# Window attention on one core: patch loads moved from Sync to GpSimd, loads of x moved from GpSimd to Sync

## The chip, the cores and the metric

The kernel runs on one core of a Trainium2 chip. The metric is the device time of one execution in microseconds (us), lower is better. The fast runs of one kernel in one batch agree (the kernel before, seven runs: 5340.21 to 5358.49 us), so times are medians, and two kernels are compared on runs made on the same chip in the same batch. A run counts as fast when it lies within 1.5 per cent of the fastest of its kernel; where a kernel was run only once, its state is unknown, and that is said. PE is the matmul engine, DVE VectorE, ACT ScalarE, POOL GpSimd and SP SyncE. SP only issues transfers here.

## The reference, cut to what matters

```python
# x: [1, 511, 511, 192] bf16, windows of 7x7 (73 x 73 = 5329 of them), 4 heads
pe = 0
for i in range(3):
    for j in range(3):
        pe = pe + xp[:, i:i+H, j:j+W, :] * dw_pe[i, j]   # depthwise 3x3, x padded by 1
x0 = x + pe
h = layernorm(x0)
qkv = windows(h) @ w_qkv                  # per window: 49 tokens x 192
out = softmax(q @ k^T * dh**-0.5) @ v     # per head
return x0 + out @ w_o
```

Of the kernel before, what the change touches and what calls it, by code (L numbers as in the profile page):

```python
# [33 lines left out]
def _window_attn_kernel(ctx: ExitStack, tc: tile.TileContext, x, dw_pe, w_qkv, w_o, out, fast=None, eps=1e-5, logit_lim=40.0):  # L34
    nc = tc.nc
# [55 lines left out]
    def segments(blk):  # L91
        n0 = blk * BLK
        n1 = min(n0 + BLK, NWIN)
        segs = []
        n = n0
        while n < n1:
            a, b0 = divmod(n, NWC)
            b1 = min(NWC, b0 + (n1 - n))
            segs.append((a, b0, b1, n - n0))
            n += b1 - b0  # L100
        return segs

    def load_xc(blk):
        xc = XC[blk % 2]
        for (a, b0, b1, p0) in segments(blk):
            for o in range(0, b1 - b0, 16):
                nb = min(16, b1 - b0 - o)
                nc.gpsimd.dma_start(  # L108
                    out=xc[p0 + o : p0 + o + nb].rearrange("p (r q) c -> p r (q c)", q=WS), in_=xw[a, b0 + o : b0 + o + nb]
                )  # L110

    def load_xp(blk):
        for (a, b0, b1, p0) in segments(blk):
            nb = b1 - b0
            if a == NWR - 1 and blk > 0:
                nc.gpsimd.memset(XP[0:KP, p0 : p0 + nb, :], 0.0)
            else:
                if b0 == 0:
                    nc.gpsimd.memset(XP[0:9, p0 : p0 + 1, :], 0.0)
                if b1 == NWC:  # L120
                    nc.gpsimd.memset(XP[64:KP, p0 + nb - 1 : p0 + nb, :], 0.0)
            pr0 = 1 if a == 0 else 0
            pr1 = 8 if a == NWR - 1 else 9
            h0 = WS * a - 1
            for pc in range(9):
                if pc == 0:
                    q, sh = WS - 1, -1
                elif pc == 8:
                    q, sh = 0, 1
                else:  # L130
                    q, sh = pc - 1, 0
                bb0, bb1 = b0, b1
                if pc == 0 and bb0 == 0:
                    bb0 = 1
                if pc == 8 and bb1 == NWC:
                    bb1 = NWC - 1
                if bb1 <= bb0:
                    continue
                nc.sync.dma_start(
                    out=XP[9 * pc + pr0 : 9 * pc + pr1, p0 + bb0 - b0 : p0 + bb1 - b0, :],  # L140
                    in_=xr[h0 + pr0 : h0 + pr1, bb0 + sh : bb1 + sh, q, :],
                )


    load_xc(0)
    load_xp(0)

    nc.gpsimd.memset(Sel, 1.0)
# [85 lines left out]
    def main(fast):  # L234
      with ExitStack() as mctx:
# [344 lines left out]
        if NBLK > 1:  # L580
            load_xp(1)
# [5 lines left out]
        for g in range(NGL + LE + 1):  # L587
# [9 lines left out]
            if ck == LE and blk >= 1:  # L597
                proj(blk - 1)
                store(blk - 1)
                if blk + 1 < NBLK:  # L600
                    load_xc(blk + 1)
# [3 lines left out]
            if nb < NBLK:  # L605
                if blk == 0 and ck == 0:
                    load_xc(nb)
# [5 lines left out]
                if ck == cend and nb + 1 < NBLK:  # L613
                    load_xp(nb + 1)
# [75 lines left out]
```

## The kernel before: the parts that the change and the argument touch

A block is 128 windows; there are 42. x is loaded twice. Once by token into `XC`, with one window on each partition (this is the x that the convolution is added to). Once as patches into `XP`: the 9x9 patch of a window lies on 81 partitions, so that the depthwise convolution is one small matmul per channel. A patch load fills nine neighbouring partitions (nine rows of the image, one column of the patch) for up to 73 windows, with 384 bytes per window and partition.

```python
def load_xc(blk):                                  # x by token, 9 or 10 loads a block
    xc = XC[blk % 2]
    for (a, b0, b1, p0) in segments(blk):
        for o in range(0, b1 - b0, 16):
            nb = min(16, b1 - b0 - o)
            nc.gpsimd.dma_start(                   # L108
                out=xc[p0 + o : p0 + o + nb].rearrange("p (r q) c -> p r (q c)", q=WS), in_=xw[a, b0 + o : b0 + o + nb])

def load_xp(blk):                                  # patches, 18 or 27 loads a block
    for (a, b0, b1, p0) in segments(blk):
        ...                                        # memsets of the edges on GpSimd (L119, L121)
        for pc in range(9):
            ...
            nc.sync.dma_start(                     # L139
                out=XP[9 * pc + pr0 : 9 * pc + pr1, p0 + bb0 - b0 : p0 + bb1 - b0, :],
                in_=xr[h0 + pr0 : h0 + pr1, bb0 + sh : bb1 + sh, q, :])

def build_D(blk, g):                               # seven of these a block
    nc.gpsimd.tensor_tensor(out=D[:], in0=ident..., in1=rstd..., op=ALU.mult)      # L327
def transposes(blk):                               # scaled by D, first work of a block
    ... nc.tensor.matmul(ps[...], lhsT=xc[...], rhs=D[:, ss, :], ...)              # L346
def conv_tile(blk, it):
    ... nc.tensor.matmul(ps[...], lhsT=XP[0:KP, :, c], rhs=T[0:KP, c, :], ...)     # L282
    ... nc.vector.tensor_tensor(out=xc..., in0=ps..., in1=xc..., op=ALU.add)       # L284

for g in range(NGL + LE + 1):                      # 16 steps ck to a block
    if ck == 0 and blk < NBLK: transposes(blk)
    ...
    if ck == LE and blk >= 1:
        proj(blk - 1); store(blk - 1)              # L396, on SP
        if blk + 1 < NBLK: load_xc(blk + 1)        # into the buffer just stored
    ...                                            # convolution of block nb = blk + 1
    if ck == cend and nb + 1 < NBLK:
        load_xp(nb + 1)                            # as soon as that convolution is done
    if ck >= cend:
        stats_part(nb, sa, sb); ...                # DVE, then rstd, then build_D(nb, ...)
```

So the order in a block is: the convolution ends; the patches of the next block may be loaded; DVE makes the statistics; POOL builds D; PE transposes; attention; the block before is stored; x is loaded into its buffer; the next convolution is added to it.

## Time and profile before

| | before |
|---|---|
| median | 5348.66 us (2 runs, 5340.74 to 5356.59) |
| PE / DVE / ACT / POOL busy | 84 / 72 / 51 / 14 % |
| period of a block | 124.5 us |
| convolution's end to first D / to first transpose | 23.5 / 27.7 us |
| first store to first addition of the convolution | 29.7 us |

The last three rows are means over some 39 blocks, read from the timelines of PE, POOL, SP and DVE: the end of the last L282 matmul of a block, the start of its first L327, of its first L346, of the first L396 after it, and of the first L284 after that. The rest of the period (transposes, attention up to the stores, and the convolution) is 67.0 us. These stages are the ruler of this study, because the change can only act at two places: between the convolution and the transposes, where POOL works, and between the stores and the additions, where x comes in.

Of PE's waits, two belong to those places: the wait for D, and that of the projections behind the first additions. The view of the waits, kernel before; the columns are engine, line, what it waited for, total us, how many times, the longest:

```profile
PE ps L412 <- DVE XC L284: 62.2, 36, 5.7
PE ps L346 <- POOL D L327: 35.8, 32, 18.9
```

Both are small: 0.9 to 1.5 us a block.

### The profile page before, as it was taken

To read this page: it belongs to the slowest core of one execution; us is meant where nothing else is said; L and a number is where in the kernel's file an instruction comes from. 1 tells how busy PE (TensorE), PEld (TensorE's weight loads), DVE (VectorE), ACT (ScalarE), POOL (GpSimd) and SP (SyncE) were. 2 spreads that over 40 slices of the span, in tenths; PEclk is the share of its full clock that TensorE was granted. 3 is DMA by queue.
4 is the path that set the end of the run, shared out by engine and by line. 5 is a ranking of instruction groups with operands and counts; after the bars stand their busy time and mean duration, and the time that the engine had idled before them with its cause. 6 is when DMAs were issued, how large, how long until landed. Compare 5 with 4: busy or idle time off the path is not lost.

```text
span 5337.2 us, 148265 instructions
## 1 busy us (share of the span) xinstructions
PE 4490.1 (84%) x65427; PEld 3661.5 (69%) x65427; DVE 3816.7 (72%) x6912; ACT 2744.5 (51%) x3385; POOL 758.0 (14%) x833
## 2 busy tenths in 40 slices
PE   2788888888888888888988888888888888888887
PEld 1666676667776676677776777767666776677776
DVE  6776777767776777777677777777777777767776
ACT  1554555545555555555555455555555555545555
POOL 1111111111111111111111111111111111111120
PEclk9887888887778887888788877788888888877888
DMA  6554445554455555554455544455555445544431
GB/s 67 51 75 70 68 71 80 82 73 68 68 68 70 71 72 74 71 74 71 68 73 91 75 68 68 68 72 72 74 72 72 73 70 78 85 74 67 68 48 32
DMA packets 512613, 375.27 MB, mean 70 GB/s; under 512 B 453129, under 2 KB 453321, under 8 KB 511958
## 3 DMA queue, kind: packets, MB, share of 16 engines
q1 hardware_dynamic: 480918, 265.08, 38.1%
q0 software_dynamic: 30592, 100.32, 10.6%
q8 instruction: 514, 8.42, 0.7%
q14 instruction: 141, 1.16, 0.1%
q10 hardware_dynamic: 448, 0.30, 0.0%
HBM read 265.31 MB, written 100.27 MB: 68 GB/s over the span
## 4 chain that ended last, share of the span: by engine, by line
PE 44%; DVE 16%; ACT 14%; DMA 12%; SPq 9%; issue 4%; POOL 1%; DVEq 0%; ACTq 0%; POOLq 0%
PE ps L412 12%; PE ps L282 8%; SPq L396 7%; DMA out_dram<-XC 7%; PE ps L369 6%; DMA XC<-in_x_dram 5%; PE ps L453 5%; PE ps L532 4%; DVE kT L424 4%; ACT hT L355 4%; DVE Qb L422 3%; PE ps L431 2%; DVE XC L284 2%; PE ps L560 2%; ACT kT L426 2%
## 5 line engine op out<-in xcount | busy, mean ns | idle before, releaser
L412 PE MATMUL ps<-hT,Wqk 96*128 96x392 bf16 x5336 | 1233.5, 380 | 76.7 <-DVE XC L284 62.2
L478 ACT ACTIVATE PT<-ps 128x784 bf16<-128x784 f32 x667 | 552.7, 829 | 1095.3 <-PE ps L453 1080.3
L421 ACT CAST Qb<-ps 64x784 bf16<-64x784 f32 x667 | 555.3, 833 | 657.5 <-PE ps L412 655.7
L412 PEld LDWEIGHTS <-Wqk 96*128 96x128 bf16 x5336 | 529.4, 108 | 486.1 <-issue 252.5
L284 DVE TENSOR_TENSOR XC<-ps,XC 128x980 bf16<-128x980 f32 x378 | 437.9, 1176 | 503.0 <-PE ps L282 247.2
L282 PE MATMUL ps<-T,XP 81*128 81x49 bf16 x8064 | 744.0, 264 | 55.5 <-DMA XP<-in_x_dram 55.5
L567 ACT CAST OT<-ps 96x784 bf16<-96x784 f32 x667 | 541.0, 811 | 456.0 <-PE ps L560 452.4
L282 PEld LDWEIGHTS <-XP 81*128 81x128 bf16 x8064 | 733.9, 220 | 57.6 <-issue 55.5
L431 PE MATMUL ps<-Wv,hT 96*128 96x192 bf16 x5336 | 663.5, 277 | 16.4 <-DVE On L544 9.0
L532 PE MATMUL ps<-V,PT 49*64 49x49 bf16 x21344 | 542.5, 195 | 159.1 <-DVE Qb L422 81.2
L431 PEld LDWEIGHTS <-hT 96*128 96x128 bf16 x5336 | 548.8, 111 | 180.0 <-issue 91.6
L544 DVE TENSOR_TENSOR On<-ps,rs 128x768 bf16<-128x768 f32 x667 | 634.6, 951 | 16.0
L532 PEld LDWEIGHTS <-PT 49*64 49x64 bf16 x21344 | 466.2, 116 | 260.4 <-issue 217.7
L327 POOL TENSOR_TENSOR D<-ident,rstd 128x896 bf16<-128x896 bf16 x294 | 486.2, 1681 | 1074.8 <-DVE rstd L320 1053.3
L424 DVE CAST kT<-ps 128x784 bf16<-128x784 f32 x462 | 450.0, 974 | 219.2 <-PE ps L412 209.1
L304 DVE BATCH_NORM_STATS2 bnst<-XC 128x6 f32<-128x192 bf16 x2058 | 600.5, 343 | 0.2
L453 PE MATMUL ps<-Qb,kT 128*64 128x98 bf16 x10672 | 408.0, 225 | 180.7 <-DVE Qb L422 132.2
L422 DVE CAST Qb<-ps 64x784 bf16<-64x784 f32 x462 | 451.6, 978 | 110.6 <-ACT Qb L421 100.1
L355 ACT CAST hT<-ps 96x896 bf16<-96x896 f32 x462 | 452.4, 1109 | 135.9 <-PE ps L346 134.9
L560 PE MATMUL ps<-ident,On 128*96 128x98 bf16 x5336 | 412.1, 226 | 114.4 <-DVE kT L424 110.9
L453 PEld LDWEIGHTS <-kT 128*64 128x64 bf16 x10672 | 341.5, 121 | 231.5 <-issue 131.7
L108 POOL DMA_DIRECT2D XC<-in_x_dram x386 | 216.0, 560 | 1865.9 <-DVE rs L543 996.3
(73 smaller groups left out, 4396.2 us busy)
## 6 DMA issues: line engine op xcount, KB each, us to landing
XC<-in_x_dram POOLq DMA_DIRECT2D x277, 294.0 KB, 7.5
out_dram<-XC SPq DMA_DIRECT2D x277, 294.0 KB
XP<-in_x_dram SPq DMA_DIRECT2D x210, 246.4 KB
XP<-in_x_dram SPq DMA_DIRECT2D x68, 243.0 KB
XC<-in_x_dram POOLq DMA_DIRECT2D x37, 165.4 KB, 7.1
out_dram<-XC SPq DMA_DIRECT2D x37, 165.4 KB
XP<-in_x_dram SPq DMA_DIRECT2D x22, 216.0 KB
XP<-in_x_dram SPq DMA_DIRECT2D x18, 212.6 KB
```

Source lines behind the costliest of these rows:

```text
L282: nc.tensor.matmul(ps[:, col : col + S], lhsT=XP[0:KP, :, c], rhs=T[0:KP, c, :], start=True, stop=True)
L304: nc.vector.bn_stats(out=bnst[:, s, :], in_=xc[:, s, :])
L355: nc.scalar.copy(out=hv[0:KT, kt, :, s0 : s0 + NDG], in_=src)
L412: nc.tensor.matmul(ps[:, ab * 512 : ab * 512 + TOK], lhsT=Wqk[kt][0:KT, which * 2 + ab, :], rhs=hT[0:KT, kt, ck * CH : (ck + 1) * CH, 0:S] ...
L421: nc.scalar.copy(out=dst[0:64, :, :, 0, :], in_=src[0:64])
L422: (nc.vector.tensor_copy if dve_help else nc.scalar.copy)(out=dst[64:128, :, :, 1, :], in_=src[64:128])
L424: nc.vector.tensor_copy(out=dst[:, :, 0:TOK], in_=two_bank(ps, TOK))
L431: nc.tensor.matmul(ps[:, col : col + C], lhsT=hT[0:KT, kt, ck * CH + 2 * jj : ck * CH + 2 * jj + 2, :].rearrange("p w s -> p (w s)"), rhs= ...
L453: nc.tensor.matmul(ps[64 * wp : 64 * wp + 64, col : col + 2 * S], lhsT=k_[:, ab, w * S : w * S + 64], rhs=q_[:, ab, w, :, :].rearrange("p ...
L478: nc.scalar.activation(out=pt[:, 0 : 16 * S].rearrange("p (b n) -> p b n", b=2), in_=two_bank(ps, 8 * S), func=ACTF.Exp, scale=scale,)
L532: nc.tensor.matmul(ps[64 * wp : 64 * wp + 64, col : col + S], lhsT=pt[64 * wp : 64 * wp + S, pc_ : pc_ + 64], rhs=v_[64 * wp : 64 * wp + S ...
L544: nc.vector.tensor_tensor(out=o_[:].rearrange("p (b j) (h d) -> p b (j h) d", b=2, d=DH), in0=ov[:, :, :, 0:DH], in1=r_[:].rearrange("p (b ...
```

## The change

Its intent: SP is held for some 50 us by the issue of each block's patch loads, while POOL is idle 86 per cent of the time. So the many narrow loads go to POOL, and the loads of x, which would otherwise queue behind them there, to SP, behind the stores that they depend on anyway.

```diff
@@ load_xc
-                nc.gpsimd.dma_start(
+                nc.sync.dma_start(
@@ load_xp
-                nc.sync.dma_start(
+                nc.gpsimd.dma_start(
```

## The prediction

> **What bounds the kernel now.** The engine shares of the page come first: no engine is full, so the time is set by waits and by the order of stages. The PE row has no clock-free reading, so I went on to the timeline.
>
> ```profile
> PE 4490.1 (84%) x65427; PEld 3661.5 (69%) x65427; DVE 3816.7 (72%) x6912; ACT 2744.5 (51%) x3385; POOL 758.0 (14%) x833
> ```
>
> PE is near the bound, POOL nearly idle. POOL idle time costs nothing now; the question is whether POOL gets onto the path.
>
> The kernel runs 42 blocks of 128 windows. The timelines of SP and POOL in the stretch 1000 to 1400 us show one block's period, 1227.28 - 1104.30 = 123 us, and when each of the moved transfers is issued.
>
> ```profile
> 1104.30 49.69 SPq L139 DMA_DIRECT2D XP<-in_x_dram  x27
> 1168.06 14.62 SPq L396 DMA_DIRECT2D out_dram<-XC  x10
> 1227.28 41.40 SPq L139 DMA_DIRECT2D XP<-in_x_dram  x27
> ```
>
> SP is held 41 to 50 us by the 27 patch loads (XP) of a block, then free until the stores. Nothing on SP waits behind them; the patches are not read before the next convolution at 1189.93.
>
> ```profile
> 1104.39 0.25 POOL L121 MEMSET XP<- 17x192 bf16 x1 [35.96 <-PE ps L282]
> ...
> 1125.51 6.61 POOL L327 TENSOR_TENSOR D<-ident,rstd 128x896 bf16<-128x896 bf16 x4 [19.97 <-DVE rstd L320]
> 1134.90 4.97 POOL L327 TENSOR_TENSOR D<-ident,rstd 128x896 bf16<-128x896 bf16 x3 [2.78 <-DVE rstd L320]
> 1172.95 0.57 POOL L108 DMA_DIRECT2D XC<-in_x_dram  x1 [33.08 <-DVE rs L543]
> ```
>
> POOL builds the seven diagonal matrices D, 1.68 us each, as soon as the statistics (rstd) are there: 21 us after the convolution ends. The PE timeline shows who needs them next.
>
> ```profile
> 1129.91 0.55 PE L346 MATMUL ps<-D,XC 128*96 128x128 bf16 x7 [0.15 <-ACT Qb L422]
> ```
>
> PE reaches the transposes at 1129.91. D number one is ready at 1125.51 + 1.68 = 1127.2: **2.7 us of slack**, no more. All of the next block's projections hang on these transposes.
>
> The chain that ended last, in order of time, shows the second place where the moved transfers matter:
>
> ```profile
> 1168.96 2.20 SPq L396
> ...
> 1181.52 8.04 DMA out_dram<-XC
> 1189.60 0.60 issue
> 1190.20 7.59 DMA XC<-in_x_dram
> 1198.58 3.35 DVE XC L284 x3
> ```
>
> The store of a finished block, then the reload of the same buffer with x, then the addition of the convolution. On PE this costs two gaps per block, 1.98 us before 1189.29 and 2.59 us before 1199.81, not the whole 30 us.
>
> [...]
>
> ```profile
> q1 hardware_dynamic: 480918, 265.08, 38.1%
> q0 software_dynamic: 30592, 100.32, 10.6%
> ```
>
> [...] during the patch loads the DMA rows say share 0.73 to 0.76 and only 63 to 94 GB/s (windows 1110 to 1150), against 288 GB/s in 1180 to 1185 when stores and x loads run together. [...] Here the 386 x loads last 533/535/707 ns (min/median/max), with 1 to 16 partitions but always 7 rows per partition. So the length doesn't grow with partitions; whether it grows with rows per partition no instruction of this kernel shows. A patch load has up to 73.
>
> **The change part by part.**
>
> Removed from SP: 1025 patch loads. This by itself gains nothing, since SP was free when the stores became ready (patch issues end at 1154, the stores start at 1168).
>
> Added to POOL: those loads, in program order between the memsets and the seven D builds. The built instruction order confirms: memset, 9 loads, two memsets, 9 loads, memset, 9 loads, then D. It also shows that each load waits for the completion of the one eight before it (eight completion semaphores in turn). So the 27th issues only when the 19th has landed, and D comes after that. Where a block has three row segments (a, 73 and 55 - a windows) the first 19 loads hold about 80% of the patches.
>
> How long is that? Three sizes:
> - *Same drain as on hardware.* 27 issues held SP 41 to 50 us; 80% of about 50 us is 40 us. POOL is free at 1104.3 + 40 = 1144, first D at 1146; PE wanted it at 1129.9. Stall 16 us per block, times 41 blocks = **+660 us**.
> - [...]
> - [...] If half of the 535 ns is fixed and half belongs to the 7 rows, a row costs 38 ns; a block has 9 x 128 = 1152 rows per partition, so 27 x 0.27 + 1152 x 0.038 = 51 us; POOL free at 1155, stall 27 us, times 41 = **+1100 us**. If nothing were fixed, 76 ns a row: 88 us, stall 64 us, +2600 us. If all is fixed: 27 x 0.54 = 15 us, no stall.
>
> Moved from POOL to SP: 386 loads of x. Before, POOL issued each as soon as its own store had landed, among SP's remaining stores (1172.95 to 1190.2). Now all ten stores are issued first, until 1168.06 + 14.62 = 1182.7, then the loads. If they take the stores' pace of 1.46 us each, the last goes out near 1197; against that, nothing competes with the stores any more[...]. Before, the last landed at 1197.8; I take 1197 to 1201 after, so 0 to 3 us per block, half of it caught elsewhere: **-50 to +120 us**, centre +40.
>
> The start: PE waits for the first patches until 109.8 us (55.5 us of wait in the row of PE). [...]
>
> Sum: I weigh the three sizes 0.30, 0.40 and 0.30 (the last between +500 and +2600), with +40 for x and -20 at the start. The mean lies near +600; I name +500: 5349 + 500 = **5850 us**.
>
> **The rivals.**
> *POOL never gets onto the path.* For it: its cadence at the start, eight x loads within 4.5 us, is 0.55 us whatever their size, and 27 such issues fit into the 21 us before rstd[...]. Against: the wait on the load eight before ties POOL to landing, not to issuing. Then 5300 to 5400.
> *The patches themselves come late for the convolution.* They have 1104 to 1190, 86 us plus any stall. [...] It would add to the same stall rather than form a new one; then 7000 and more. I give it one in twelve.
> *The x loads decide.* If SP's order makes them 5 us later, that is +200 us with POOL innocent; if hardware loads are so quick that both gaps of PE close, 4.6 us times 41 = -190 us, the only way to be faster by over 2%. The store time of 1.46 us each speaks against the latter.
> [...] the small statistics operation L309, 0.19 us at 1120, lasts 1.42 us at 1129 while POOL builds D. Loads now overlap the statistics; I allow some us per block within the range.
>
> **How the range and the chances follow.** Low 5300: spread, no stall, start gained. High 6550: 1100 us of stall plus 100 us for x. Below and above one chance in ten. Slower by over 2% (above 5456) needs 2.6 us of stall per block beyond the slack: 0.70. Within 2%: 0.24. Faster: 0.06.
>
> **What would show it.** In the profile after, the POOL timeline between the last convolution matmul and the first D: if this is 20 us or less the first rival holds; if 40 us, the drain[...]. PE L346 should have idle time ended by POOL D, of stall times 41. POOL's DMA rows should show 1025 loads, their length against 535 ns. SP's L108 should start at the end of the stores. The prediction is wrong if L346 waits little while the time rises, or if the added wait is at L282 or L284 instead.

Two terms of the forecast's sum rested above all on how many DMA engines a load would use: the second of the three sizes (weight 0.40, no stall, 0 us; "spread" under the range) and the reason for the -20 us at the start. The sum came to 0.30 x 660 + 0.40 x 0 + 0.30 x some 1300 = some 590 us for D, plus 40 for x, less 20 at the start: some 610, of which it named +500. Without the two terms, and with the weights as they stand, it is some 630 us. The third size assumes that the length of an issuing instruction on POOL grows with the rows; that was an estimate from the 535 ns of the loads of x. "Software" and "hardware" loads, here and in the expectations, are those of the queues that the page calls software_dynamic (issued by POOL) and hardware_dynamic (issued by SP).

## The result, and the profile after

The kernel after takes 6407.27 us (2 runs, 6396.35 to 6418.20) against 5348.66: **1.197 times** the time, with a 95% interval of 1.190 to 1.204; 1058.6 us slower. A ratio here is the mean time of one kernel's fast runs over that of the other's of the same rounds, so it isn't quite the ratio of the medians. The time lies within the predicted range, but the change is twice the predicted +500.

The page's own sections 1 and 4, kernel after: engine shares, then the chain that ended last, by engine.

```profile
PE 4704.1 (73%) x65427; PEld 3805.0 (59%) x65427; DVE 3766.1 (59%) x6912; ACT 2767.8 (43%) x3385; POOL 1297.8 (20%) x1472
...
PE 38%; DMA 35%; DVE 12%; POOL 8%; issue 3%; ACT 2%; SPq 0%; DVEq 0%; POOLq 0%; ACTq 0%
```

The same chain line of the kernel before:

```profile
PE 44%; DVE 16%; ACT 14%; DMA 12%; SPq 9%; issue 4%; POOL 1%; DVEq 0%; ACTq 0%; POOLq 0%
```

DMA went from 12 to 35 per cent of the chain: the end is now set by transfers. Which ones, the waits tell (kernel after, columns as above):

```profile
POOL XP L139 <- DMA XP<-in_x_dram: 1054.2, 482, 7.0
...
PE ps L346 <- POOL D L327: 527.4, 139, 46.8
...
DVE XC L284 <- DMA XC<-in_x_dram: 301.3, 40, 11.5
PE ps L412 <- DVE XC L284: 271.1, 40, 10.7
```

POOL waits 1054 us inside its own sequence of patch loads for earlier patch loads to land. PE's wait for D rose from 36 to 527 us, and its wait behind the first additions from 62 to 271 us. So both places got longer. One block on POOL, kernel after (timeline: start, us, engine, line, what, how many; in brackets the idle time before and what ended it):

```profile
1316.62 5.36 POOL L139 DMA_DIRECT2D XP<-in_x_dram  x9 [0.28 <-issue]
...
1322.51 6.80 POOL L139 DMA_DIRECT2D XP<-in_x_dram  x8
1331.03 0.85 POOL L139 DMA_DIRECT2D XP<-in_x_dram  x1 [1.71 <-DMA XP<-in_x_dram]
...
1356.00 0.71 POOL L139 DMA_DIRECT2D XP<-in_x_dram  x1 [4.76 <-DMA XP<-in_x_dram]
...
1359.52 11.53 POOL L327 TENSOR_TENSOR D<-ident,rstd 128x896 bf16<-128x896 bf16 x7
```

The first 17 loads go out at once, at 0.6 to 0.85 us each. From there each load waits until the one eight before it has landed: over the run, 464 of POOL's 475 such waits over 0.3 us end within 0.75 us of that landing. D, ready to be built some 21 us after the convolution in the kernel before, starts 43 us after it here (1316.1 to 1359.5). All seven D then follow without a gap: the statistics were long there. PE in the same stretch, same view:

```profile
1342.98 0.84 PE L532 MATMUL ps<-V,PT 49*64 49x49 bf16 x23 [5.73 <-issue]
...
1361.26 4.21 PE L346 MATMUL ps<-D,XC 128*96 128x128 bf16 x42 [12.74 <-POOL D L327]
```

Two things are to be seen: the wait of 12.74 us for D, and before it a pause of 5.73 us in the middle of one group of matmuls, for which the profile shows no releaser ("issue"). I come back to the pause below.

The second place is the reload of x. SP issues in one run; then comes the chain, kernel after, two views:

```profile
1250.35 13.99 SPq L396 DMA_DIRECT2D out_dram<-XC  x10
1264.44 8.12 SPq L108 DMA_DIRECT2D XC<-in_x_dram  x9
```

```profile
1272.29 15.81 DMA XC<-in_x_dram
1288.18 3.35 DVE XC L284 x3
```

The last load goes out at 1272.3, 22 us after the first store, which is as early as before (1168.06 to 1190.2 there). But it lands 15.8 us later, where before it took 7.6 (the prediction's lines have the chain of before).

The ruler, kernel before against after:

| mean us per block | before | after | difference |
|---|---|---|---|
| convolution's end to first D | 23.45 | 45.39 | |
| convolution's end to first transpose | 27.74 | 47.73 | +20.0 |
| first store to first addition | 29.72 | 37.26 | +7.5 |
| the rest | 67.0 | 66.2 | -0.8 |
| period | 124.47 | 151.15 | +26.7 |

Over 41 blocks, 20.0 us make 820 us and 7.5 us make 309. PE's one wait for the first patches fell from 55.5 to 42.1 us, a gain of 13 us. The sum 820 + 309 - 34 - 13 = 1082 us stands against a difference of the two profiled spans of 6416.5 - 5337.2 = 1079.3 us. So the time is placed. "The rest" is as long as before although the mean granted clock of PE is lower over the run (0.75 after, 0.82 before), so I count the clock as no cause of its own here.

### The profile page after: what moved, and what is told of

The parts are those of the page before. It is cut to its first block, busy times and chain, and to the rows that moved or that the text cites. A ratio compares the mean times of both kernels' runs of the same rounds, so it can differ in the third digit from the quotient of the medians.

```text
span 6416.5 us, 147155 instructions
## 1 busy us (share of the span) xinstructions
PE 4704.1 (73%) x65427; PEld 3805.0 (59%) x65427; DVE 3766.1 (59%) x6912; ACT 2767.8 (43%) x3385; POOL 1297.8 (20%) x1472
## 3 DMA queue, kind: packets, MB, share of 16 engines
q0 software_dynamic: 93168, 166.16, 31.5%
q14 instruction: 132, 1.08, 0.1%
## 4 chain that ended last, share of the span: by engine, by line
PE 38%; DMA 35%; DVE 12%; POOL 8%; issue 3%; ACT 2%; SPq 0%; DVEq 0%; POOLq 0%; ACTq 0%
DMA XP<-in_x_dram 21%; DMA XC<-in_x_dram 14%; PE ps L412 11%; PE ps L282 7%; POOL D L327 6%; PE ps L369 5%; DVE kT L424 5%; PE ps L532 4%; PE ps L453 4%; DVE Qb L422 3%; POOL XP L139 2%; PE ps L560 2%; DVE XC L284 2%; PE ps L431 2%; PE ps L377 1%
## 5 line engine op out<-in xcount | busy, mean ns | idle before, releaser
L412 PE MATMUL ps<-hT,Wqk 96*128 96x392 bf16 x5336 | 1340.6, 402 | 316.6 <-DVE XC L284 271.1
L412 PEld LDWEIGHTS <-Wqk 96*128 96x128 bf16 x5336 | 558.4, 113 | 761.9 <-issue 562.3
L139 POOL DMA_DIRECT2D XP<-in_x_dram x1025 | 758.1, 746 | 1074.2 <-DMA XP<-in_x_dram 1054.2
L282 PE MATMUL ps<-T,XP 81*128 81x49 bf16 x8064 | 752.7, 262 | 96.9 <-DVE On L544 54.0
L282 PEld LDWEIGHTS <-XP 81*128 81x128 bf16 x8064 | 744.1, 217 | 102.1 <-issue 93.1
L121 POOL MEMSET XP<- 17x192 bf16 x72 | 18.1, 251 | 3771.2 <-PE ps L282 3770.0
L346 PE MATMUL ps<-D,XC 128*96 128x128 bf16 x4116 | 364.3, 257 | 566.7 <-POOL D L327 527.4
L532 PE MATMUL ps<-V,PT 49*64 49x49 bf16 x21344 | 568.3, 199 | 225.1 <-issue 101.0
L431 PE MATMUL ps<-Wv,hT 96*128 96x192 bf16 x5336 | 699.4, 287 | 40.5 <-issue 31.0
L431 PEld LDWEIGHTS <-hT 96*128 96x128 bf16 x5336 | 576.5, 115 | 219.9 <-issue 137.2
L346 PEld LDWEIGHTS <-XC 128*96 128x96 bf16 x4116 | 340.4, 155 | 594.9 <-issue 569.2
L422 DVE CAST Qb<-ps 64x784 bf16<-64x784 f32 x462 | 451.5, 977 | 348.2 <-ACT Qb L421 337.7
L304 DVE BATCH_NORM_STATS2 bnst<-XC 128x6 f32<-128x192 bf16 x2058 | 600.5, 343 | 0.4
L453 PE MATMUL ps<-Qb,kT 128*64 128x98 bf16 x10672 | 427.1, 230 | 231.1 <-DVE Qb L422 132.6
```

Source lines behind the costliest of these rows:

```text
L139: nc.gpsimd.dma_start(out=XP[9 * pc + pr0 : 9 * pc + pr1, p0 + bb0 - b0 : p0 + bb1 - b0, :], in_=xr[h0 + pr0 : h0 + pr1, bb0 + sh : bb1 + ...
L282: nc.tensor.matmul(ps[:, col : col + S], lhsT=XP[0:KP, :, c], rhs=T[0:KP, c, :], start=True, stop=True)
L304: nc.vector.bn_stats(out=bnst[:, s, :], in_=xc[:, s, :])
L346: nc.tensor.matmul(ps[0:KT, ss * 128 : (ss + 1) * 128], lhsT=xc[:, s0 + ss, kt * KT : (kt + 1) * KT], rhs=D[:, ss, :], start=True, stop=True,)
L412: nc.tensor.matmul(ps[:, ab * 512 : ab * 512 + TOK], lhsT=Wqk[kt][0:KT, which * 2 + ab, :], rhs=hT[0:KT, kt, ck * CH : (ck + 1) * CH, 0:S] ...
L422: (nc.vector.tensor_copy if dve_help else nc.scalar.copy)(out=dst[64:128, :, :, 1, :], in_=src[64:128])
```

## The experiments

My theory after the result: (1) POOL can't build D until its patch loads have nearly all landed, and they land no faster from POOL than they did from SP (from the first issue of a block to its last patch packet, by the packet records, 52.0 us on the mean against 54.7 before); this is the 20 us. (2) The loads of x start later (13.2 us after the first store instead of 5.4), and take some 24 us from there, as before; this is the 7.5 us. Rivals: issuing from POOL limits the pace of the patch loads; the loads of x are slow because SP issues them; the loads from POOL slow other engines.

In all, twelve kernels ran; all passed the comparison with the reference. "Before" is each time the kernel before in the same batch.

### Each half alone

```diff
 e_patch_only: L139 nc.sync -> nc.gpsimd, L108 left on nc.gpsimd
 e_x_only:     L108 nc.gpsimd -> nc.sync, L139 left on nc.sync
```

> Only the patch loads move to GpSimd; the x loads stay there as before. Theory (two separate costs per block: first diagonal build 20 us later, x loads 7.5 us later): the time is 5349 + 41 x 20 = about 6170 us, convolution's end to first transpose matmul 48 us, first store to first addition still 30 us. Rival (the two moves act together, or the x loads make the most of it): below 5800 or back near 6400.

> Only the x loads move to Sync; the patch loads stay there as before. Theory: 5349 + 41 x 7.5 = about 5660 us, first store to first addition 37 us, convolution's end to first transpose 28 us as before. Rival (the x loads are late only because software patch loads are about): within 1% of 5349.

Patch loads alone: 6100.00 us against 5350.50, ratio 1.1415 (1.1386 to 1.1445). Loads of x alone: 5638.45, ratio 1.0543 (1.0497 to 1.0589). The two add up: +749.5 and +288.0 are 1037.5, against 1058.6 for both. The stages keep apart too. With the patch loads alone the first transpose comes 47.13 us after the convolution and the remainder of the period is 96.2 us (before: 96.7). With the loads of x alone the first transpose comes after 28.44 us, but the first addition 37.47 us after the first store. So the two halves are two independent costs.

### D ahead of the patch loads

The kernel after, with the patch loads of a block emitted behind its last D:

```diff
-                if ck == cend and nb + 1 < NBLK:
-                    load_xp(nb + 1)
 ...
                             for gg in range(4, NG):
                                 build_D(nb, gg)
 ...
+                        if nb + 1 < NBLK:
+                            load_xp(nb + 1)
```

> The changed kernel, with the patch loads emitted after the diagonal builds on GpSimd, so the builds no longer stand behind them. Theory (the builds wait because GpSimd is held by the wait for the load eight before): convolution's end to first transpose falls from 48 to 26-28 us, time about 5660 us; up to 150 us more if the patch loads, now later, meet the stores and x loads. Rival [...]: stays above 6000 us.

Measured: 6093.99 us, ratio 1.1401 (1.1370 to 1.1433). The wait for D is gone: first D 22.94 us and first transpose 26.62 us after the convolution, better than before the change. That shows the first half of theory (1): POOL's program order is what made D late. But the time fell by only some 310 us from the kernel after's 6407. In number this is the rival's (above 6000 us). But its reason, that the loads from POOL slow DVE or the building of D wherever they run, doesn't show: one D takes 1.68 us and one L304 of the statistics 0.34 us, as before. POOL's timeline of this kernel (columns as above):

```profile
2122.98 6.60 POOL L327 TENSOR_TENSOR D<-ident,rstd 128x896 bf16<-128x896 bf16 x4 [20.46 <-DVE rstd L320]
...
2137.28 5.40 POOL L139 DMA_DIRECT2D XP<-in_x_dram  x7
```

D waits for the statistics again, as it should, and the patch loads start behind it. The price is a new one, on PE in that time:

```profile
2159.78 0.34 PE L377 MATMUL ps<-XC,ident 128*128 128x192 bf16 x1 [5.43 <-issue]
...
2186.18 0.41 PE L532 MATMUL ps<-V,PT 49*64 49x49 bf16 x8 [4.49 <-issue]
```

PE stops for 4 to 5 us, with no releaser in the profile. Added over the run such pauses of PE come to 333 us here, 288 us in the kernel after and 263 us with the patch loads alone, but 32 us in the kernel before and 50 us with the loads of x alone (sums of PE's waits ended by "issue"). In the kernel after they lie mostly in time that PE would have waited for D anyway; with D first they lie on the path, and the stretch from the transposes' end to the first store grows from 26.4 to 36.4 us. Of these 10 us the pauses are 6.7; the rest is PE busy for longer (27.4 against 24.3 us), with a granted clock of 0.72 and 0.50 in the windows 2160 to 2170 and 2190 to 2200, just behind the two pauses. So with the slow drain of patch loads from POOL goes a second effect, which moving D doesn't cure.

What do these pauses wait for? The packet records say something: of the kernel after's 55 pauses over 2 us, every one ends 1.5 to 3.6 us after the end of a 16 KB packet on the queue that the page lists as "instruction" (514 packets), while only about one moment in five, taken over the run, lies as close behind such a packet. With D first all 65 do (1.3 to 3.6 us). The longest pause of the kernel after is 9.9 us. So the pauses go with those packets. Why PE stops until just after one of them, no run shows.

### Why the drain is slow: half the bytes, and other partitions

The windows view of both kernels in the middle of a patch stage (us, its length, busy time and count of PE, PEld, DVE, ACT and POOL, PE's clock, the DMA engines' busy share, GB/s). Before:

```profile
1110.00:1120.00 10.00, 8.69 (x154) 6.47 (x152) 9.40 (x31) 9.88 (x14) 0.00 (x0) 1.00 0.75 64
1120.00:1130.00 10.00, 8.34 (x155) 6.47 (x154) 9.50 (x40) 9.88 (x14) 4.49 (x3) 1.00 0.76 63
```

After:

```profile
1330.00:1340.00 10.00, 5.95 (x92) 4.33 (x90) 8.19 (x37) 8.39 (x12) 2.50 (x4) 1.00 1.08 79
1340.00:1350.00 10.00, 5.55 (x67) 4.03 (x68) 4.59 (x20) 4.52 (x6) 2.13 (x3) 0.66 1.02 76
```

From POOL the engines' share rises from about 0.75 to between 1.02 and 1.08. (The trace doesn't name the engines, and packets overlap in time, as a share above 1 shows, so the share doesn't count them.) But they move 76 to 79 GB/s here and 77 on the mean of the patch stages, hardly more than the 63 to 81 of before (four such windows from 1110 to 1150; 60 to 96 in windows of 5 us) and its mean of 73. The share of the engines is high and little is moved. Two candidates: the number of runs of 384 bytes that a load brings, whatever their length, or the place where the data lands, nine neighbouring partitions. That the place counts was my guess; no trace had shown it so far. Two edits of the kernel after separate the candidates. The first moves half the channels in every patch load, a wrong kernel (it passes the comparison all the same, probably because the reference draws the convolution's weights very small, 0.005):

```diff
-  out=XP[9 * pc + pr0 : 9 * pc + pr1, p0 + bb0 - b0 : p0 + bb1 - b0, :],
-  in_=xr[h0 + pr0 : h0 + pr1, bb0 + sh : bb1 + sh, q, :],
+  out=XP[9 * pc + pr0 : 9 * pc + pr1, p0 + bb0 - b0 : p0 + bb1 - b0, 0:96],
+  in_=xr[h0 + pr0 : h0 + pr1, bb0 + sh : bb1 + sh, q, 0:96],
```

The second brings the same rows by the same loads, but puts row r, column c of a patch on partition 9r + c instead of 9c + r, with the weights and the edge memsets to match:

```diff
-  dwK[9 * j : 9 * j + 3, :] <- dw_pe[:, j, :]          # in short
+  dwK[9 * j : 9 * j + 3, :] <- dw_pe[j, :, :]
-  pattern=[[-1, WS], [-9, WS], [1, KP]],
+  pattern=[[-9, WS], [-1, WS], [1, KP]],
-  nc.gpsimd.memset(XP[0:9, ...], 0.0)  and  (XP[64:KP, ...], 0.0)
+  nc.gpsimd.memset(XP[0:KP, ...], 0.0)
-  out=XP[9 * pc + pr0 : 9 * pc + pr1, ...],
+  out=XP[9 * pr0 + pc : 9 * (pr1 - 1) + pc + 1 : 9, ...],
```

> The changed kernel, each patch load brings only the first 96 of 192 channels: as many loads and runs, half the bytes; the output is wrong on purpose. Theory (a run of the load costs the same whatever its length): GpSimd still starts the diagonal builds 45 us after the convolution's end and the time stays within 3% of 6407 us. Rival (bytes set the drain): the builds start 27 to 32 us after, time about 5800 us.

> The changed kernel, with patch row r of column c on partition 9r+c instead of 9c+r, so one load writes nine partitions nine apart instead of nine neighbours; the result stays right. Theory A [...]: builds start 27 to 35 us after the convolution's end, time 5700 to 5900 us. Theory B (the cost lies on the side of the 384-byte reads): 45 us and 6400 us as in the changed kernel.

Half the bytes, one look of unknown state: 5787.36 us; first D after 28.77 us instead of 45.39, PE's pauses 145 us. So the theory that a run costs the same whatever its length fell. The queue table of this kernel (queue, kind, packets, MB, share of 16 engines):

```profile
q0 software_dynamic: 60384, 83.78, 20.1%
```

That is 0.201 x 5785.6 = 1163 us of all sixteen engines. (The packets are fewer too, so this edit alone doesn't separate bytes from packets.) Rows spread: 5705.87 us, ratio 1.0683 (1.0636 to 1.0731); first D after 28.09 us, first transpose after 30.59, PE's pauses 19 us, first convolution matmul at 78.9 us instead of 96.4. The same windows view, rows spread:

```profile
1430.00:1440.00 10.00, 8.49 (x152) 6.47 (x152) 9.40 (x34) 9.88 (x14) 7.00 (x10) 1.00 1.04 139
1440.00:1450.00 10.00, 7.89 (x144) 5.81 (x144) 9.30 (x43) 9.88 (x14) 3.65 (x7) 1.00 1.05 140
```

Same share of the engines, 139 to 140 GB/s instead of 76 to 79, and PE and ACT nearly as busy as before the change. The queue table makes it exact. Kernel after, then rows spread:

```profile
q0 software_dynamic: 93168, 166.16, 31.5%
```

```profile
q0 software_dynamic: 93168, 166.16, 19.3%
```

The packets and the bytes are the same to the digit. The engines' time is not: 0.315 x 6416.5 = 2021 us of all sixteen engines against 0.193 x 5705.1 = 1101 us, or 48 against 26 us per block; a block's patches drain in 31.9 us instead of 52.0. The loads are as long to issue as before (0.55 to 0.88 us each by size, in both). So neither the count of packets nor the time of issuing on POOL sets the pace of the patch loads; the destination partitions do. (From SP, in the kernel before, the trace records some 429,000 packets of 384 bytes for the same patches, against the 93,168 of all sizes from POOL, and the pace is about the same: 73 and 77 GB/s.) What it is about the partitions, no run separates.

### What is left with both cures

```diff
 e_rows_spread with the edit of e_d_first on top
```

> The changed kernel with both remedies: partitions of a patch load nine apart, and patch loads emitted after the diagonal builds. Theory [...]: first transpose 26 to 28 us after the convolution's end, TensorE's waits for nothing seen below 50 us in all, first store to first addition still 37 us, time 5340 + 41 x 7.5 less 20 to 30 us at the start = about 5620 us. Rival (software loads cost something more wherever they run): 5700 us or more.

Measured: 5657.12 us, ratio 1.0564 (1.0524 to 1.0604). First D after 22.58 us, first transpose after 26.32, PE's pauses about 21 us in all. What remains of the change's cost is the later x: first addition 37.66 us after the first store. The ratio is near that of the loads of x alone, 1.0543, with overlapping intervals, and the period of a block is the same (132.7 and 132.6 us). So POOL's order and the slow drain explain the cost of the patch loads, as far as these runs can tell.

### The loads of x: when they start, or who issues them

Four kernels bear on it. `e_x_interleave` is the kernel before with the loads of x on SP, each behind the store four places further on instead of behind all stores. `e_x_late_sw` and `e_x_late_hw` make all loads of x wait for all stores, by a tiny memset over the whole buffer's partitions ahead of them, and issue them from POOL and from SP. `e_x_reverse` was meant to make the loads from POOL late by reversing their order.

```diff
 e_x_interleave:
-                store(blk - 1); load_xc(blk + 1)
+                for i in range(max(len(sts), len(lds) + 4)):
+                    if i < len(sts): sts[i]()             # one store, SP
+                    if 4 <= i < len(lds) + 4: lds[i - 4]()  # one load of x, SP
 e_x_late_sw and e_x_late_hw (the latter also L108 -> nc.sync):
                 if blk + 1 < NBLK:
+                    nc.gpsimd.memset(XC[(blk + 1) % 2][:, 0, 0:2], 0.0)
                     load_xc(blk + 1)
 e_x_reverse:
-        for (a, b0, b1, p0) in segments(blk):
-            for o in range(0, b1 - b0, 16):
+        for (a, b0, b1, p0) in reversed(segments(blk)):
+            for o in reversed(range(0, b1 - b0, 16)):
```

> Patch loads on Sync as before; x loads on Sync too, but each emitted four places behind its own store instead of after all stores. Theory (x loads are late because all stores stand ahead of them): first store to first addition 30 us or less, time 5350 us or up to 2% less. Rival (hardware x loads themselves are slower than software ones): 37 us and 5660 us as with x loads last.

> The kernel before, its x loads still on GpSimd, but issued in reverse order, so the first one waits for the last store to land. Theory (x loads take some 24 us from first issue to last landing on either queue, and what counts is when the first can start): first store to first addition about 20 + 24 = 44 us, time about 5349 + 41 x 14 = 5900 us. Rival (hardware x loads are slower in themselves than software ones): 27 to 33 us, within 3% of 5349 us.

> The kernel before, with a two-element memset on GpSimd over all partitions of the buffer ahead of the x loads, so the software x loads start only when the last store has landed (the reversed order of the last batch was undone by the scheduler). Theory (software and hardware x loads drain alike; the start counts): first store to first addition 42 to 46 us, time 5850 to 6000 us, and the same as the hardware twin within 1%. Rival (hardware x loads are slower): 5 us or more shorter than the twin.

> The same memset ahead of the x loads issued from Sync, patch loads on Sync as before. Theory: same as its software twin, 42 to 46 us from first store to first addition. Rival (hardware loads slower): longer than the twin by 5 us or more per block, 200 us or more in time.

The reversal failed as an experiment: 5346.87 us, ratio 0.9989 (0.9933 to 1.0044), because the scheduler put the loads back into nearly the old order (in the block looked at, only the last two are exchanged); the first load still went out 5 us after the first store. It tells nothing of the question.

The late pair, one look each, of unknown state: 5769.90 us from POOL, 5821.35 us from SP. The first addition comes 40.9 and 41.7 us after the first store, a little less than expected. POOL's part of the software one, timeline (L601 is the memset):

```profile
1267.22 0.10 POOL L601 MEMSET XC<- 128x2 bf16 x1 [44.79 <-DMA out_dram<-XC]
1267.87 4.31 POOL L108 DMA_DIRECT2D XC<-in_x_dram  x8 [0.54 <-POOL XC L601]
```

Its first store is issued at 1250.64, so the loads start 17.2 us later here. Means over some 39 blocks, in us:

| | before | after | x alone on SP | late, POOL | late, SP |
|---|---|---|---|---|---|
| first store to first load | 5.4 | 13.2 | 13.1 | 18.2 | 17.6 |
| first load to first addition | 24.3 | 24.1 | 24.4 | 22.7 | 24.2 |

Where all loads go out together, behind the stores, the burst takes 23 to 24 us, and who issues it makes 1.5 us; so what counts is when it starts. The theory that loads of x are slower from SP falls. The 24.3 us of the kernel before are not such a burst: there each load waits for its own store, and the chain runs through the landing of the last store and then of the last load (8.04 and 7.59 us in the prediction's lines). That the two agree is partly chance.

Interleaving gives 5503.28 us, ratio 1.0298 (1.0258 to 1.0338): it wins back about half of the cost, with the first addition 33.88 us after the first store, where 30 us or less was expected. It doesn't win back all: the first load goes out early (6.6 us after the first store), but the addition follows only 27.3 us later. SP in this kernel, timeline (L406 a store, L417 a load of x):

```profile
2739.51 5.58 SPq L406 DMA_DIRECT2D out_dram<-XC  x5
...
2758.65 4.85 SPq L417 DMA_DIRECT2D XC<-in_x_dram  x4
```

The stores of the block need 19 us to go out (2739.5 to 2758.5), where they took 14.6 in the kernel before. That stores and loads on SP wait for each other is how I read this; no run tests it.

One more, of a suspicion that the partitions limit this burst as they do the patches: the kernel before with the chunks of 16 windows spread over the partitions.

```diff
-                out=xc[p0 + o : p0 + o + nb]...      in_=xw[a, b0 + o : b0 + o + nb]
+                out=xc[p0 + o : p0 + e : m]...       in_=xw[a, b0 + o : b0 + e : m]     # m windows apart; stores alike
```

> The kernel before with each store and x load taking 16 windows as far apart as the segment allows instead of 16 neighbours. Theory [...]: first store to first addition falls from 30 to 25 us or less, the two gaps of TensorE close, time 5150 to 5250 us. Rival [...]: 30 us and 5348 us within 1%; or longer, since each load now waits for four stores.

Measured: 5330.01 us, ratio 0.9970 (0.9931 to 1.0010); first addition 29.93 us after the first store. No net effect, but two changes cancel: the first load goes out 8.6 us after the first store instead of 5.4 (each load now waits for several stores), and the addition follows 21.4 us after it instead of 24.3. So the choice of partitions isn't ruled out as what limits the burst to 2.41 MB (128 x 49 x 192 x 2 bytes) in some 24 us, about 100 GB/s; spread chunks issued all together weren't tried, and it stays open.

### A version that beats both

The rows spread took a block's drain from 52.0 to 31.9 us with the loads issued by POOL. So the kernel before got them too, with the loads left on SP.

```diff
 e_rows_spread_hw: before.py with the edit of e_rows_spread, L139 left on nc.sync
```

> The kernel before with the nine partitions of each patch load nine apart, loads still on Sync. Theory [...]: the 27 patch loads hold Sync 30 us or less instead of 41 to 50; the time stays within 1% of 5348 us, since patch loads aren't on the path there. Rival [...]: 41 to 50 us as before.

Measured: 5290.64 us (5272.22 to 5317.59) against 5342.06, ratio **0.9876** (0.9836 to 0.9917): 1.2 per cent faster than the kernel before (clear of noise, but under the 2 per cent at which these studies call a kernel faster) and some 17 per cent below the 6407.27 us that the kernel after took in its own batch. SP and one window of its patch stage:

```profile
1197.02 28.30 SPq L139 DMA_DIRECT2D XP<-in_x_dram  x27
...
1322.92 30.93 SPq L139 DMA_DIRECT2D XP<-in_x_dram  x27
```

```profile
1205.00:1215.00 10.00, 9.32 (x149) 6.74 (x148) 8.08 (x28) 9.62 (x13) 0.00 (x0) 0.89 0.63 160
```

Over the run, SP is held for 27 to 32 us by the 27 loads of a block (mean 29) instead of 41 to 62 (mean 51), and the window shows 160 GB/s. The gain is small, because with the loads on SP the patches were hidden already: the period is as before (124.5 us), and 23 us come at the start, where the first convolution matmul runs at 86.8 instead of 109.8 us. The other part of the 51 us lies within the spread of the runs and I don't assign it.

## Why the prediction was right or wrong, point by point

**Direction and mechanism of the patch loads: right.** The prediction had D late behind POOL's patch loads, through the wait for the load eight before, and named its place: L346 waiting for POOL D. That wait rose from 35.8 to 527.4 us, and putting D first removed it. Two readings beside it were off. PE's first transpose in the block shown runs at 1129.20, not 1129.91, so D had 2.0 us of slack there and not 2.7; this is small. And the gap of 1.98 us before 1189.29 is ended by the cast of q (DVE Qb L422), not by x: this wait is 81.2 us in 41 times before and 79.3 us in 40 times after, so only the second gap was x's.

**The sizes of the drain: this step failed.** The largest weight, 0.40, stood on the second size: the loads were to drain faster from POOL, so that there was no stall. That was an estimate, and no trace had shown it. The engines' share did rise (from about 0.75 to between 1.02 and 1.08), but the pace hardly did: 76 to 79 GB/s, and a block's patches drain in 52.0 us instead of 54.7. The runs showed that the destination partitions limit a patch load: 139 to 140 GB/s at about the same share (1.04 to 1.05) with the rows spread. The weight should have gone to "Same drain as on hardware", which gave a stall of 16 us and +660 us; the measured stall is 20.0 us and 820 us. The missing 4 us: the step had POOL free 40 us after the convolution, and on the mean the first D came after 45.4 us. The third size was wrong as well: 38 ns per row (a window, in a patch load) was a guess from one kind of load, and the trace shows 0.56 us for loads of 2 windows, 0.60 to 0.65 for 16 to 18 and 0.86 for 73, about 4 ns each. Group L139 of the page, kernel after, has the mean:

```profile
L139 POOL DMA_DIRECT2D XP<-in_x_dram x1025 | 758.1, 746 | 1074.2 <-DMA XP<-in_x_dram 1054.2
```

758 us over 41 blocks are 18.5 us a block, which would have fitted into the 21 us before rstd. So the sum of weights had 0.30 x some 1300 us = 390 us for a cost that isn't there, and for the stall that is there 0.30 x 660 us only. The upper end of the range, too, was built on this third size; that the measured time lies below it is luck in part.

**The loads of x: mechanism named, size wrong by a factor of eight.** The prediction took 0 to 3 us per block, +40 us; it measured 7.5 us and +309 us. This step failed too: it followed the last load's issue, near 1197, and let the landing come 0 to 4 us behind, though its own line has 7.59 us from issue to landing. In fact the last load went out about as early as before (22 us after the first store in the blocks shown, not 29), but landed 15.8 us later instead of 7.6: the burst as a whole started 7.8 us later on the mean and took its 24 us from there. The rival "The x loads decide" had the number, +200 us for 5 us, but not the weight. This term is the largest single miss of the sum: 270 us.

**The start: right in sign, 13 us against the 20 of the sum.**

**Patches late for the convolution, DVE slower beside the loads from POOL: neither happened in a way that these runs show.** L282's wait on patches in the kernel after is the 42.1 us at the start, once. DVE's busy time is 3766 us, 50 below that of before.

**Not foreseen: PE's pauses**, 288 us in the kernel after. They cost little there, it seems, since PE had to wait for D, but became 6.7 us a block on the path once D came in time. They go with the slow drain from POOL: 288 us where it runs at 76 to 79 GB/s, 19 us when the same packets drain at 139 to 140 GB/s, and none with the rows spread and the loads on SP. They end just behind instruction packets, as said above; why, is not shown.

Summed: -13 at the start, 820 for D, 309 for x, and -34 for the rest (0.8 us a block, which I don't assign), where the prediction had -20, a mean of some 590, and 40, and then named 500, some 110 below its own sum.

## What to carry to other kernels

A transfer that moves to an engine with computing to do brings its wait for landing along (here POOL waited 1054 us for landings, and the first D came 45 us after the convolution instead of 23): read how long the loads take to drain, not how long they take to issue, and put the engine's computing ahead of them in program order. Don't take a higher share of the DMA engines for a higher pace: here, with nine neighbouring partitions to a load, the share rose from about 0.75 to between 1.02 and 1.08, and the pace only from 63 to 81 GB/s to 76 to 79 (means 73 and 77). Try a layout in which each load strides over the partitions; here it took the drain from 52 to 32 us a block. Where loads wait for stores in the same buffer, ask when the first of them can go out, and not only the last: issued between the stores from another queue, they let the addition start 7.5 us earlier here than behind all of them.
